# One written order for all engines and the loads, natural rows transposed by TensorE, and a shorter conversion of the weights

## The chip, the cores and the metric

The kernel runs on one core of a Trainium2 chip. The core has TensorE (PE in the profile, with its weight loads as PEld), VectorE (DVE), ScalarE (ACT), GpSimd (POOL) and SyncE (SP), which here only issues DMA transfers. The metric is the device time of one execution in microseconds (us), lower is better. A second execution with the hardware profiler gives the trace.

## The reference

Two attentions in a row, then a two-layer network with a softmax-weighted activation and a layer norm. B = 8 batches, H = 8 heads, S = 576 positions, D = 64, 32 packed rows of p for each head.

```python
def sm_attn(qq, kk, vv):
    s = scale * np.matmul(qq, kk.transpose(0, 1, 3, 2))
    s = s - np.max(s, axis=-1, keepdims=True)
    a = np.exp(s)
    a = a / (np.sum(a, axis=-1, keepdims=True) + 1e-09)
    return np.matmul(a, vv)
p_packed = sm_attn(p, k, v)
out = sm_attn(q, p_packed, p_packed)
# x: out with the heads side by side, 4608 tokens x 512
h = x @ w_in                       # 512 x 1024
e = np.exp(h - np.max(h, axis=-1, keepdims=True))
solu = h * (e / (np.sum(e, axis=-1, keepdims=True) + 1e-09))
ln = (solu - mean) / np.sqrt(var + 1e-06) * g_ln
return (ln @ w_out).astype(np.float32)   # 1024 x 512
```

`w_in`, `w_out` and `g_ln` are used here as they come: the two weight matrices lie in memory as float64, q, k, v, p and `g_ln` as float32. The output is float32.

## The kernel before

**Batches.** Each batch has two halves of attention. `pack(b)` (L342 on) computes the packed rows: k is transposed to `kT`, scores against p's transpose (L360 for batch 0, L368 later), softmax (L371 to L386), transposes of the weights `e1` by TensorE (L397), the product with v (L407, called PV here), the division by the row sums (`pp`, L411) and a transpose to `ppT` (L413, L415). `unpack(b)` computes the attention of q on those rows: q is transposed to `qT` (L428, by DVE in 32x32 blocks, or for batches 0 and 1 by TensorE in `transpose_rows`), scores (L457, L467), transposes of score blocks (L439), softmax (L443 to L451, two of its steps, L444 and L451, on POOL for b ≥ 1). The product with p's rows and the product with `w_in` are taken together: z = `ppT` times `w_in` (L483), split into a rounded part `zh` (L485) and the rest `zl` (L500, or for batch 0 L491 and L493 on ACT and POOL). The weights of the second attention are transposed (L505) and split the same way into `a2h` (L507) and `a2l` (L508).

**Token tiles.** 36 tiles of 128 tokens. `mlp_in` (L521) adds three products for each half (`a2h·zh + a2h·zl + a2l·zh`): 12 matmuls of 128x512, or 24 for the tile that lies across two batches. Then row maximum (L523), exponential (L531), `u` (L534); `mlp_norm` subtracts the mean (L542), writes `yhl` as two float16 parts (L544 on ACT, L545 on DVE), transposes them by DMA into `yT` (L547), and gets the row factor `c_row` (L549 to L555). `mlp_out` is 24 float16 matmuls into `po` (L564) with `w_out` as two float16 parts `wch` and `wcl`; the row and column factors go on in L566, and L571 stores.

**Weights.** Both matrices come as pairs of 32-bit words in chunks of 1 MB, four for each matrix. `high_part` (L202 on ACT, L204 and L205 on DVE) makes a float32 from the high words: the exponent is rebased by a scaling and a shift, and the sign bit is put back from the source by L205. `add_low_part` adds what the low words hold (L212 takes the power of two, L217, or L220 and L221, the product, L226/L227 or L233 the sum; a table `HOW` chooses engines for each of the eight chunks; in two ways, `3` and `6`, TensorE adds the parts in PSUM). For `w_out`, magnitudes are summed over rows (L301, L302), giving a power-of-two column scale (L307 to L311); each of eight chunks of 128 rows is multiplied by `g_ln` and that scale (L321, L322) and split into `wch` (L323) and `wcl` (L330).

**Loads.** Everything goes through SP's one queue. k of later batches is loaded in blocks with pieces of 128 bytes (L96), q in blocks too (L85); rows of k, q (batches 0 and 1) and v go in pieces of 512 bytes (L107) and a tail of 64 rows (L115 and its like). p is loaded in blocks twice: for batch 0 (L159; transposed by DVE, L261), and for the others (L167; transposed by DVE, L269, then four copies from SBUF to SBUF, L272).

**Start.** TensorE runs 12 small fp32 matmuls on ones (L248) and, at a few places, runs of 128x512 matmuls on ones (`keep_busy`, L255), 22 of which are before k's transposes.

**What sets the order.** For batches 1 to 7 TensorE's order is the order of the code, with positions taken from the tables `FIRST_BATCH` and `LATER` (`manual_schedule` for TensorE alone). All else is placed by a scheduler, which goes by estimated times and by the priority offsets in the tables at the top. Buffers: `raw` 3, `v_sb` 1, two each of `e`, `u`, `yhl`, `yT`, `o_sb`; PSUM 2 of `h`, 1 of `po`, 3 of `pa`.

## Time and profile before

| | |
|---|---|
| time, median of 3 runs | 469.91 us (468.54 to 470.03) |
| the profiled execution's own time | 468.75 us |
| its span in the trace | 466.9 us |
| PE busy | 429.6 us, 92% |
| DVE busy | 355.1 us, 76% |
| ACT busy | 231.2 us, 50% |
| POOL busy | 143.4 us, 31% |
| TensorE's mean granted clock | 0.952 |
| moved by DMA | 67.00 MB, 143 GB/s |

The shares are means over very different stretches: the page's slices show TensorE at 5 to 9 tenths in the first third and at 9 from then to the last slice, and DVE full from about the fifth slice to the tenth. The span is cut by stretch in the prediction. In a row of the trace, "x40" is the number of instructions of a group; an fp32 matmul leaves two records.

### The profile page before, as it was taken

The page shows a single profiled execution, that of the slowest core. Times are in us where ns is not written, and L with a number is a line of the kernel's source. Part 1 is how long each engine was busy: PE and PEld are TensorE (multiplying, and loading weights), DVE is VectorE, ACT ScalarE, POOL GpSimd, SP SyncE. Part 2 cuts the span into 40 slices and gives each one's busy share as a digit, 9 for nine tenths or more (in the row PEclk, how much of TensorE's full clock was granted, in tenths as well). Part 3 has the DMA queues.
Part 4 walks back from the last instruction along what each step waited for, and adds up shares of the span by engine and source line. Part 5 has one row for each costly group of instructions (what it writes and reads, how often), then busy time and mean ns, then how long its engine had stood idle before and what let it go on. Part 6 is the DMA issues. An engine that isn't in the chain of part 4 may idle for free.

```text
span 466.9 us, 8257 instructions
## 1 busy us (share of the span) xinstructions
PE 429.6 (92%) x3116; PEld 236.3 (51%) x3116; DVE 355.1 (76%) x649; ACT 231.2 (50%) x403; POOL 143.4 (31%) x243
## 2 busy tenths in 40 slices
...
GB/s 267 338 268 286 155 191 132 128 184 173 153 103 186 142 97 160 224 128 157 176 140 144 97 155 183 77 119 178 69 67 69 76 62 113 90 67 125 80 115 65
DMA packets 237880, 67.00 MB, mean 143 GB/s; under 512 B 208912, under 2 KB 231440, under 8 KB 237328
## 3 DMA queue, kind: packets, MB, share of 16 engines
...
q14 instruction: 16, 0.13, 0.1%
...
## 4 chain that ended last, share of the span: by engine, by line
PE 38%; DVE 31%; ACT 9%; issue 7%; DMA 7%; POOL 4%; SPq 2%; DVEq 0%; POOLq 0%; ACTq 0%
PE po L564 21%; PE h L521 12%; DVE nm L523 4%; ACT yhl L544 3%; DMA zh<-in_moe_w_in_dram 3%; DVE qT L428 3%; DVE kT L350 3%; DVE u L534 3%; DVE zl L500 3%; ACT e L549 2%; DVE yhl L545 2%; DVE mx L443 2%; DVE sm L448 2%; PE pa L407 1%; PE pa L467 1%
## 5 line engine op out<-in xcount | busy, mean ns | idle before, releaser
L564 PE MATMUL po<-wch,yT 128*128 128x512 f16 x576 | 182.7, 382 | 5.9 <-DVE o_sb L566 4.8
L564 PEld LDWEIGHTS <-yT 128*128 128x128 f16 x864 | 81.0, 98 | 115.2 <-issue 24.7
L564 PE MATMUL po<-wcl,yT 128*128 128x512 f16 x288 | 109.7, 381 | 0.0
L521 PE MATMUL h<-zh,a2h 128*128 128x512 f32 x160 | 70.2, 439 | 1.8 <-DVE u L534 1.5
L531 ACT ACTIVATE e<-h,nm 128x1024 f32<-128x1024 f32 x36 | 40.1, 1115 | 58.1 <-DVE nm L523 57.6
L544 ACT ACTIVATE yhl<-u,negmu 128x1024 f16<-128x1024 f32 x36 | 41.4, 1149 | 50.9 <-POOL negmu L542 47.2
L521 PE MATMUL h<-zh,a2l 128*128 128x512 f32 x160 | 64.4, 403 | 0.0
L521 PE MATMUL h<-zl,a2h 128*128 128x512 f32 x160 | 64.2, 401 | 0.0
L545 DVE SCALAR_TENSOR_TENSOR yhl<-u,negmu,yhl 128x1024 f16<-128x1024 f32 x36 | 46.4, 1288 | 17.4 <-ACT yhl L544 17.3
L534 DVE SCALAR_TENSOR_TENSOR u<-e,s_row,h 128x1024 f32<-128x1024 f32 x36 | 46.0, 1277 | 9.8 <-ACT e L531 8.6
L523 DVE TENSOR_REDUCE nm<-h 128x1 f32<-128x1024 f32 x36 | 43.6, 1212 | 11.7 <-PE h L521 11.6
L566 DVE SCALAR_TENSOR_TENSOR o_sb<-po,c_row,inv 128x512 f32<-128x512 f32 x36 | 26.8, 745 | 26.1 <-PE po L564 26.1
L551 POOL TENSOR_SCALAR s_eps<-se,s_row 128x1 f32<-128x1 f32 x36 | 10.7, 297 | 102.2 <-ACT e L531 65.3
L554 POOL TENSOR_SCALAR c_row<-sq,s_eps 128x1 f32<-128x1 f32 x36 | 15.7, 437 | 82.9 <-ACT e L549 82.9
L549 ACT ACTIVATE e<-u,negmu 128x1024 f32<-128x1024 f32 x36 | 40.9, 1136 | 0.0
L521 PEld LDWEIGHTS h<-zh,a2h 128*128 128x128 f32 x160 | 31.1, 194 | 18.9 <-issue 9.0
L521 PEld LDWEIGHTS h<-zh,a2l 128*128 128x128 f32 x160 | 30.8, 193 | 7.9 <-issue 0.5
L521 PEld LDWEIGHTS h<-zl,a2h 128*128 128x128 f32 x160 | 31.1, 194 | 6.0
L444 POOL TENSOR_TENSOR s<-s,mx 128x576 f32<-128x576 f32 x14 | 16.0, 1160 | 49.3 <-DVE mx L443 49.3
L446 ACT ACTIVATE a<-s 128x576 f32<-128x576 f32 x16 | 10.9, 684 | 30.6 <-POOL s L444 28.1
L508 DVE TENSOR_TENSOR a2l<-s,a2h 128x576 fp32r<-128x576 f32 x16 | 14.0, 881 | 13.1 <-ACT a2h L507 13.1
L381 ACT ACTIVATE e<-pa,nmx 128x288 f32<-128x288 f32 x28 | 13.7, 496 | 19.4 <-DVE nmx L373 10.8
(139 smaller groups left out, 614.1 us busy)
## 6 DMA issues: line engine op xcount, KB each, us to landing
...
```

What stands on the lines that cost most here:

```text
L350: nc.vector.transpose(out=kT[:, g], in_=kraw[:, g].rearrange('p a i -> p (a i)'))
L444: eng.tensor_tensor(out=s2[r], in0=s2[r], in1=mx.unsqueeze(2).broadcast_to([P, NB, J]), op=ALU.subtract)
L521: nc.tensor.matmul(h[:, 512 * n:512 * n + 512], lhsT=lhsT, rhs=z[:, r, 512 * n:512 * n + 512], start=t == 0, stop=t == len(terms) - 1)
L523: nc.vector.tensor_reduce(out=nm, in_=h, axis=AX.X, op=ALU.max, negate=True)
L531: nc.scalar.activation(e, h, AF.Exp, bias=nm, accum_out=se)
L534: nc.vector.scalar_tensor_tensor(out=u, in0=e, scalar=s_row, in1=h, op0=ALU.mult, op1=ALU.mult, accum_out=su)
L544: nc.scalar.activation(yhl[:, 0], u, AF.Identity, bias=negmu)
L545: nc.vector.scalar_tensor_tensor(out=yhl[:, 1], in0=u, scalar=negmu, in1=yhl[:, 0], op0=ALU.add, op1=ALU.subtract)
L549: nc.scalar.activation(e, u, AF.Square, bias=negmu, accum_out=sq)
L554: nc.gpsimd.tensor_scalar(out=c_row, in0=sq, scalar1=1.0 / DF, scalar2=s_eps, op0=ALU.mult, op1=ALU.add)
L564: nc.tensor.matmul(po, lhsT=yT[:, a, c], rhs=w[:, c], start=c == 0 and t == 0, stop=c == NFC - 1 and t == 2)
L566: nc.vector.scalar_tensor_tensor(out=o_sb, in0=po, scalar=c_row, in1=inv, op0=ALU.mult, op1=ALU.mult)
```

## The change

1. **One region with a written order.** All tables of offsets go. Every stage is a generator that emits one step at each call, and a string of about 1,300 names says which generator is called next. All engines, and SP's loads, follow that order. `Z` is the warm-up, `lk0` a load, `W0` and `O0` the conversion of a chunk, `S` the column scale, `C0` the scaled parts of a chunk, `k0` and `q0` the two halves of a batch, `z0` its z, `t0` a token tile.
2. **Natural rows.** k of batch 0 and q of batches 0 and 1 are loaded as rows with four positions of a head together (pieces of 1 KB), v of all batches as well; TensorE transposes k and q, and the two tails go by two 128x128 transposes. p is loaded once, as rows, and transposed by TensorE; ACT scales and copies it.
3. **Sign by slope.** `high_part` uses ACT's Prelu with a slope of 2^32 for negative inputs, so that one shift by DVE leaves the sign bit in place, and L205 falls away. The power of two for the low part comes from the same bits.
4. **Parts added by TensorE.** For all eight chunks of the conversion the low and high parts are added in PSUM (`whole`). Seven of the eight scaled chunks of `w_out` go from PSUM through one DVE instruction that applies `g_ln` and the column scale; the other takes ACT and POOL.
5. **Engines.** Tables choose POOL or DVE for the low products, the rests `zl`, `a2l`, `wcl` and two softmax steps. Runs of fill matmuls after the start are gone; the warm-up is 24 small and 15 large matmuls.

```diff
-HOW = '42313324'
-SCALED_BY = 'pppppdpp'
-REST_BY = 'pdddppdd'
+HOW = 'pddddddd'
+SCALED_BY = 'xxxxxxpx'
+REST_BY = 'ppppddpd'
+ZL_BY = 'ppdppdddpdpddddddddddddddddddddd'
+A2L_BY = 'pdpddpdddddddddd'
+SOFT_BY = 'dppppppppppppppp'
+KPE = '10000000'
+QPE = '11000000'
+ORDER = 'Z lk0 lw0 W0 W0 lw1 W0 lw3 lp lw2 W0 W0 lo1 lq0 lo0 k0 k0 k0 k0 k0 k0 k0 k0 k0 lo2 W1 W0 k0 p p p p p p p W2 ...
...
-    for _ in range(12):
-        ps = ps_a.tile([P, 512], F32, name='pa')
-        nc.tensor.matmul(ps[:, :P], lhsT=ones_f, rhs=ones_f, start=True, stop=True)
+    def warm_up():
+        for _ in range(24):
+            nc.tensor.matmul(spare[:, :P], lhsT=ones_f, rhs=ones_f, start=True, stop=True)
+        for _ in range(15):
+            nc.tensor.matmul(spare, lhsT=ones, rhs=ones.unsqueeze(1).broadcast_to([P, DM // P, P]), start=True, stop=True)
+        yield
...
+    def load_p():
+        raw = got['p'] = mlp.tile([P, DF], F32, name='e', bufs=2)
+        nc.sync.dma_start(raw[:, :ROWS // P * D], p.rearrange('b h t d -> (b h t) d')[:ROWS].rearrange('(p x) d -> p (x d)', p=P))
+        yield
+    def prepare_p():
...
+        for x0 in range(0, N, 4):
+            pt = ps_h.tile([P, DF], F32, name='h')
+            for x in range(x0, min(N, x0 + 4)):
+                for r in range(2):
+                    nc.tensor.matmul(pt[64 * r:64 * r + 64, (x - x0) * P:(x - x0 + 1) * P], lhsT=raw[:, x], rhs=ident, start=True, stop=True)
+            yield
+            n = min(N, x0 + 4) - x0
+            nc.scalar.activation(dst[:, x0:x0 + n], pt[:, :n * P].rearrange('p (x s) -> p x s', x=n), AF.Copy, scale=SCALE)
+            yield
...
     def high_part(dst, raw):
         bits = mlp.tile([P, DF], F32, name='e', bufs=2)
-        nc.scalar.activation(bits, hi.bitcast(F32), AF.Copy, scale=2.0 ** (-112))
-        bits = bits.bitcast(I32)
-        nc.vector.tensor_scalar(out=bits, in0=bits, scalar1=3, scalar2=2147483647, op0=ALU.logical_shift_left, op1=ALU.bitwise_and)
-        return nc.vector.scalar_tensor_tensor(out=dst.bitcast(I32), in0=hi, scalar=-2147483648, in1=bits, op0=ALU.bitwise_and, op1=ALU.bitwise_or)
+        nc.scalar.activation(bits, hi.bitcast(F32), AF.Prelu, scale=2.0 ** (-112), alpha=2.0 ** 32)
+        yield
+        nc.vector.tensor_scalar(out=dst.bitcast(I32), in0=bits.bitcast(I32), scalar1=3, scalar2=None, op0=ALU.logical_shift_left)
+        yield
+        return bits
+    def low_part(bits, raw, how, rest):
+        lo, _ = words_of(raw)
+        if how != 'd':
+            nc.scalar.activation(lo.bitcast(F32), lo.bitcast(U32), AF.Copy, scale=2.0 ** (-52))
+            yield
+        nc.vector.tensor_scalar(out=bits.bitcast(I32), in0=bits.bitcast(I32), scalar1=3, scalar2=-8388608, op0=ALU.logical_shift_left, op1=ALU.bitwise_and)
+        yield
+        if how == 'd':
+            nc.vector.scalar_tensor_tensor(out=rest, in0=lo.bitcast(U32), scalar=2.0 ** (-52), in1=bits, op0=ALU.mult, op1=ALU.mult)
+        else:
+            EN(nc, how).tensor_tensor(out=rest, in0=lo.bitcast(F32), in1=bits, op=ALU.mult)
+        yield
+    def whole(high, rest, i):
+        half = slice(512 * i, 512 * i + 512)
+        ps = ps_a.tile([P, 512], F32, name='pa')
+        nc.tensor.matmul(ps, lhsT=ident, rhs=high[:, half], start=True, stop=False)
+        nc.tensor.matmul(ps, lhsT=ident_r, rhs=rest[:, half], start=False, stop=True)
+        return ps
...
+    def scaled_parts(c):
+        n, i = c // 2, c % 2
+        w = wg[n][:, i * DM:(i + 1) * DM]
+        if SCALED_BY[c] == 'x':
+            ps = whole(wg[n], rests[n], i)
+            yield
+            nc.vector.scalar_tensor_tensor(out=w, in0=ps, scalar=g_sb[:, c:c + 1], in1=scale[0], op0=ALU.mult, op1=ALU.mult)
+        else:
+            EN(nc, SCALED_BY[c]).tensor_tensor(out=w, in0=w, in1=scale[0], op=ALU.mult)
+        yield
+        nc.scalar.copy(wch[:, c], w)
...
-    with tc.manual_schedule(engines={mybir.EngineType.PE}):
-        for b in range(1, B):
-            batch(b)
...
+    with tc.manual_schedule():
+        for name in ORDER.split():
+            next(flows[name], None)
```

What stands where on the engines before and after, at three places. In these rows a line number is that of the kernel's own source, a number behind a name tells buffers apart, and "x4" means four alike in a row.

TensorE at the start, before: the warm-up on ones (L248), the fill matmuls (L255), k's transposes (L125, L127).

```order
L248 MATMUL pa<-ones_f 128x128 x3
L255 MATMUL po<-ones 128x512 x15
L248 MATMUL pa<-ones_f 128x128 x3
L255 MATMUL po<-ones 128x512 x7
L125 MATMUL h<-ident,raw 64x128 x6
L248 MATMUL pa<-ones_f 128x128 x3
L125 MATMUL h<-ident,raw 64x128 x4
L127 MATMUL h<-ident,raw 128x64
```

The same place after: the warm-up (L92, L94), k's transposes (L293, L299), sums of parts of `w_in` (L203 and L204 are the two matmuls of `whole`), p's transposes (L162).

```order
L92 MATMUL po<-ones_f 128x128 x24
L94 MATMUL po<-ones 128x512 x15
L293 MATMUL h<-ident,raw 64x128 x32
L299 MATMUL h<-ident,raw 128x128 x2
L203 MATMUL pa<-w_in_sb,ident 128x512
L204 MATMUL pa<-u,ident_r 128x512
L162 MATMUL h<-ident,e 64x128 x32
```

The warm-up now stands in one piece ahead of k's transposes, and a part of `w_in` and all of p stand between these and batch 0's scores (L324, nine rows further on).

VectorE around the column scale, before: L307 to L311 compute the scale from the sums of magnitudes in `po`; L371 and L373 are batch 1's softmax maxima, L508 is `a2l` of batch 0.

```order
L350 STREAM_TRANSPOSE kT<-raw 128x576 x4
L217 SCALAR_TENSOR_TENSOR u<-raw,u 128x1024
L508 TENSOR_TENSOR a2l_183<-s_532,a2h_182 128x576
L508 TENSOR_TENSOR a2l_183<-s_536,a2h_182 128x576
L307 TENSOR_SCALAR o_sb<-po 128x512
L371 TENSOR_REDUCE mx_718<-pa 128x1 x2
L371 TENSOR_REDUCE mx_737<-pa 128x1
L308 TENSOR_SCALAR o_sb<-o_sb 128x512
L373 TENSOR_REDUCE nmx<-mx_718 128x1
L310 TENSOR_SCALAR o_sb<-o_sb 128x512
L311 TENSOR_SCALAR inv<-o_sb 128x512
L322 TENSOR_TENSOR yT<-yT,o_sb 128x512
```

After: L245 to L250 are the scale, L259 the scaled chunks that DVE reads from PSUM, L306 transposes of k of batch 1, L437 of batch 0's weights, L466 the last `zl` on DVE.

```order
L466 TENSOR_TENSOR zl<-h,zh 128x512
L437 STREAM_TRANSPOSE s_621<-a_564 128x576
L245 TENSOR_SCALAR o_sb<-po 128x512
L246 TENSOR_SCALAR o_sb<-o_sb 128x512
L248 TENSOR_SCALAR o_sb<-o_sb 128x512
L250 TENSOR_SCALAR inv<-o_sb 128x512
L259 SCALAR_TENSOR_TENSOR yT<-pa,g_sb,o_sb 128x512
L306 STREAM_TRANSPOSE kT<-raw 128x576 x2
L259 SCALAR_TENSOR_TENSOR yhl<-pa,g_sb,o_sb 128x512
L259 SCALAR_TENSOR_TENSOR yT<-pa,g_sb,o_sb 128x512
```

The four steps of the scale stand together now, and the scaling that was POOL's (seven of eight L322) is in DVE's list between them and batch 1.

SP's first loads, before: w (`zh`, `zl`, L138), p of batch 0 (L159), rows of k (L107, L115) and v.

```order
L138 DMA zh<-in_moe_w_in_dram 128x2048
L159 DMA o_sb<-in_p_dram 32x4x32 x4
L107 DMA raw<-in_k_dram 128x8x128 x2
L115 DMA raw<-in_k_dram 64x4x64 x2
L138 DMA zl<-in_moe_w_in_dram 128x2048
L107 DMA v_sb<-in_v_dram 128x8x128 x2
L134 DMA v_sb<-in_v_dram 64x8x64
L138 DMA zh<-in_moe_w_in_dram 128x2048
L138 DMA zl<-in_moe_w_in_dram 128x2048
L107 DMA raw<-in_q_dram 128x8x128 x2
```

After: k first (L102, L110), then w (L139), p whole (L149), and v of batch 0 behind q and three chunks of `w_out`.

```order
L102 DMA raw<-in_k_dram 128x8x256
L110 DMA raw<-in_k_dram 64x4x64 x2
L139 DMA zh<-in_moe_w_in_dram 128x2048
L139 DMA zl<-in_moe_w_in_dram 128x2048 x2
L149 DMA e<-in_p_dram 128x1024
L139 DMA zh<-in_moe_w_in_dram 128x2048
L139 DMA zh<-in_moe_w_out_dram 128x2x1024
L102 DMA raw<-in_q_dram 128x8x256
L110 DMA raw<-in_q_dram 64x4x64 x2
L139 DMA raw<-in_moe_w_out_dram 128x2x1024 x2
L102 DMA v_sb<-in_v_dram 128x8x256
```

`v` has moved from fourth to eleventh place, k to the first.

More of the change, by code (lines that the diff above doesn't have):

```diff
@@ L189, in packed_attention_solu_kernel @@
     wcl = const.tile([P, NFC, DM], F16, name='wcl')
[L191 to L233 removed]
+    inv = const.tile([P, DM], F32, name='inv')
     ident = const.tile([P, P], F32, name='ident')
@@ new lines, in packed_attention_solu_kernel, with raw_tile @@
+    got, packed, wg, rests, sums, scale = ({}, {}, {}, {}, [], [])
+    spare = ps_o.tile([P, DM], F32, name='po')
+    def warm_up():
[4 more added lines that the diff above has]
+        yield
+    def raw_tile():
+        return raws.tile([P, G, NB, 32], F32, name='raw', bufs=3)
@@ new lines, in whole, with convert_w_in @@
+    def whole(high, rest, i):
[4 more added lines that the diff above has]
+        return ps
+    def convert_w_in(g):
+        bits = yield from high_part(w_in_sb[:, g], got[f'w{g}'])
+        rest = mlp.tile([P, DF], F32R, name='u', bufs=2)
+        yield from low_part(bits, got[f'w{g}'], HOW[g], rest)
+        for i in range(2):
+            ps = whole(w_in_sb[:, g], rest, i)
+            yield
+            nc.scalar.copy(w_in_sb[:, g, 512 * i:512 * i + 512], ps)
+            yield
@@ L565, in mlp_out @@
         o_sb = mlp.tile([P, DM], F32, name='o_sb', bufs=2)
         nc.vector.scalar_tensor_tensor(out=o_sb, in0=po, scalar=c_row, in1=inv, op0=ALU.mult, op1=ALU.mult)
-        stores.append((out[row:row + P, :], o_sb))
-    def store():
-        while stores:
-            nc.sync.dma_start(*stores.pop(0))
-    def run(work, n=None, offset=0):
-        with tc.high_priority(offset=offset):
-            for _ in range(n or 99):
-                next(work, None)
-    work = pack(0)
-    for offset in PACK0:
-        run(work, 1, offset)
@@ L602, in packed_attention_solu_kernel @@
-    for what in 'kvq':
-        prefetch(1, what, 0)
-    pack1 = pack(1)
-    keep_busy(*BUSY[3])
-    normed, summed, stores = ([], [], [])
-    def step(row, parts, knobs, work):
-        lag, pout, pnorm = knobs
-        before, after, mid = work
-        before()
-        nxt = mlp_in(row, parts)
-        after()
-        ready = normed.pop(0) if len(normed) > lag else None
-        if summed:
-            with tc.high_priority(offset=pnorm):
-                normed.append(mlp_norm(*summed.pop()))
-        store()
-        if ready:
-            with tc.high_priority(offset=pout):
-                mlp_out(*ready, mid)
-        else:
-            for i in range(3):
-                mid(i)
-        summed.append(nxt)
@@ L627, in batch @@
-    def batch(b):
-        ui, pi, qi, (pun, patt), order, pfirst = FIRST_BATCH if b == 0 else LATER[(b - 1) % 2] if b < B - 1 else LATER[2]
-        second = unpack(b + 1) if b + 1 < B else iter(())
-        first = pack(b + 2) if b + 2 < B else iter(())
+        yield
+        nc.sync.dma_start(out[row:row + P, :], o_sb)
+        yield
+    flows = {'Z': warm_up(), 'p': prepare_p(), 'S': column_scale(), 'lp': load_p(), 'lg': load_g()}
+    for i in range(4):
+        flows[f'W{i}'] = convert_w_in(i)
+        flows[f'O{i}'] = convert_w_out(i)
+        flows[f'lw{i}'] = load_w('w', i)
+        flows[f'lo{i}'] = load_w('o', i)
@@ L636, in more @@
-        def more(n):
-            if n in qi:
-                run(pack1, qi.count(n), pfirst)
-            if n in ui:
-                run(second, ui.count(n), pun)
-            if n in pi:
-                run(first, pi.count(n), patt)
-        def at(i):
-            return (lambda: more(5 * i), lambda: more(5 * i + 1), lambda j: more(5 * i + 2 + j))
-        for i, (row, parts) in enumerate(tiles):
-            if b == 0:
-                keep_busy(*BUSY[4 + i])
-            for what, when, offset in FETCH[0 if b == 0 else 1 if b == 1 else 2]:
-                if when == i:
-                    prefetch(b + 2, what, offset)
-            step(row, parts, order, at(i))
@@ L653, in batch @@
[L653 to L664 removed]
+            flows[f't{n}'] = token_tile(n, b * S + i * P + (LEFT if odd else 0), [(odd, i * P + (P if odd else 0))])
```

549 lines of the change are left out of this document (221 added, 328 removed).

## The prediction

> **What bounds the kernel now.** I read the busy time by stretch first. Its columns are the stretch and its length in us, then busy time and count for PE, PEld, DVE, ACT and POOL, the granted TensorE clock, the DMA share and GB/s.
>
> ```profile
> 0.00:40.00 40.00, 34.16 (x333) 23.94 (x334) 21.51 (x39) 22.16 (x42) 11.54 (x16) 0.91 0.97 280
> 40.00:126.82 86.82, 67.36 (x457) 33.90 (x456) 77.81 (x117) 51.32 (x91) 48.55 (x44) 0.82 1.17 172
> 126.82:160.00 33.18, 28.91 (x248) 15.77 (x246) 22.80 (x49) 12.97 (x25) 5.50 (x12) 0.90 0.88 145
> 160.00:440.00 280.00, 277.82 (x1987) 152.42 (x1987) 223.28 (x432) 138.94 (x239) 73.82 (x163) 1.00 0.63 120
> ```
>
> From 160 to 440 TensorE is busy 277.82 of 280 us at a clock of 1.00: nothing is to be had there, and the change leaves those matmuls as they are. The tail behind it has the same last tiles. What can move is the first third. There DVE is the full engine: 77.81 of 86.82 us between 40 and 126.82. The chain of waits (start, length, what) shows which work that is, and the timeline of TensorE shows where it ends:
>
> ```profile
> 66.46 2.80 POOL yT L233
> ...
> 75.60 4.49 POOL yT L322 x3
> ...
> 413.69 5.20 PE po L564 x24
> ```
>
> ```profile
> 126.82 0.58 PE L521 MATMUL h<-zh,a2h 128*128 128x512 f32 x1
> ```
>
> The first two pieces are the middle of the chain, the conversion of `w_out` on POOL: its sums (L233) and its scaling (L322), which the first token tiles wait for. The third is one tile's `mlp_out` late in the run, where TensorE follows TensorE. I cut the run at 126.82, the first matmul that reads batch 1's `a2h`: before it TensorE mostly waits for what DVE and POOL prepare, after it it mostly works. I call that point X. In the written order of the changed kernel, the same matmul has 60 matmuls of `mlp_out` before it where this one has had 67; every other matmul ahead of it is the same work. So the sum is: DVE's work to X, plus its idle time to X, plus what is left after X.
>
> **DVE's work up to X.** Now 21.51 + 77.81 = 99.3 us. The rows (min/median/max or busy and mean in ns) that price what goes and comes:
>
> ```profile
> L205 DVE SCALAR_TENSOR_TENSOR w_in_sb<-zl,e 128x1024 int32<-128x1024 int32 x2 | 2.5, 1226 | 0.1
> ...
> L217 DVE SCALAR_TENSOR_TENSOR u<-zl,u 128x1024 f32<-128x1024 uint32 x1 | 1.2, 1225 | 0.0
> ...
> L221 DVE TENSOR_TENSOR u<-u 128x1024 f32<-128x1024 f32 x2 | 3.5, 1764 | 0.1
> ...
> L566 DVE SCALAR_TENSOR_TENSOR o_sb<-po,c_row,inv 128x512 f32<-128x512 f32 x36 | 26.8, 745 | 26.1 <-PE po L564 26.1
> ...
> L322 DVE TENSOR_TENSOR yT<-yT,o_sb 128x512 f32<-128x512 f32 x1 | 1.8, 1773 | 0.0
> ...
> L500 DVE TENSOR_TENSOR zl<-pa,zh 128x512 fp32r<-128x512 f32 x4 | 2.6, 682 | 1.0 <-ACT zh L485 1.0
> ...
> L428 DVE STREAM_TRANSPOSE qT<-raw 128x576 f32<-128x576 f32 x4 | 2.7, 734 | 0.0
> ...
> L545 DVE SCALAR_TENSOR_TENSOR yhl<-u,negmu,yhl 128x1024 f16<-128x1024 f32 x4 | 5.4, 1353 | 4.8 <-ACT yhl L544 4.8
> ...
> L269 DVE STREAM_TRANSPOSE p2t<-p2raw 128x896 f32<-128x896 f32 x1 | 1.1, 1111 | 0.8 <-ACT p2raw L267 0.8
> ...
> L508 DVE TENSOR_TENSOR a2l<-s,a2h x16: 731/746/2898, 66.3 to 415.3; 128x576 fp32r<-128x576 f32 x16
> ...
> L330 DVE TENSOR_TENSOR wcl<-yhl,wch x4: 674/1164/1429, 78.2 to 93.5; 128x512 f16<-128x512 f32 x4
> ```
>
> - Sign by slope: the eight L205 go, 8 × 1.22 = −9.8. A Prelu takes the place of the Copy on ACT, off the path (51 of 86.8 us busy); no row shows its time, and I take the Copy's, about 1.15. Twice that would add 9 us to ACT, which has over 30 to spare.
> - Low parts: seven products come to DVE and two L217 and two L221 go: 7 × 1.22 − 2 × 1.22 − 2 × 1.2 (L221 at L217's time for the same size; the rest of its 1.76 counts as contention) = +3.7.
> - Scale: seven of eight chunks are now one DVE instruction that reads the sum in PSUM. No row shows it; the nearest is L566, with the same tile, two factors and a PSUM input, 0.745. 7 × 0.75 − 0.75 for the one L322 that DVE had = +4.5. If it took L205's 1.22 it would be +3.3 more; both ends are kept.
> - `wcl` from five on DVE to three, 2 × 0.67 (L330's shortest) = −1.3; two L451 to POOL, 2 × 0.75 as L508's median for a tile of the same size, −1.5; `a2l` and `zl` of the first two batches, four of eight to POOL, −1.5 − 1.4; `p` no longer transposed here −1.7 (1.11 and two small ones); `minus_r` −0.3.
> - Moved behind X: batch 2's four q transposes, 4 × 0.73 = −2.9, and one L545, −1.3.
>
> Sum −13.5 us. The second saving is contention. Some of DVE's rows are stretched where POOL works at the same time:
>
> ```profile
> 40.00:97.00 57.00, 41.73 (x292) 22.86 (x291) 54.33 (x73) 37.20 (x68) 39.22 (x28) 0.76 1.17 171
> ...
> L204 DVE TENSOR_SCALAR e<-e x8: 653/694/2350, 7.5 to 50.5; 128x1024 int32<-128x1024 int32 x8
> ...
> L205 DVE SCALAR_TENSOR_TENSOR yT<-raw,e x2: 1224/2209/3194, 33.7 to 46.1; 128x1024 int32<-128x1024 int32 x2
> ...
> L449 DVE TENSOR_SCALAR sm<-sm x16: 131/164/1721, 54.2 to 379.6; 128x18 f32<-128x18 f32 x16
> ```
>
> Longest less median for L204, L508 and L449, longest less shortest for L205, and four times median less shortest for L330: 1.66 + 2.15 + 1.56 + 1.97 + 1.96 = 9.3 us, beside 39.2 us of POOL between 40 and 97, or 0.24 us for each us of POOL. The change takes the products L221, sums L233 and seven L322 off POOL and leaves or brings:
>
> ```profile
> L493 POOL TENSOR_TENSOR zl<-o_sb,zh 128x512 fp32r<-128x512 f32 x4 | 6.2, 1566 | 1.8 <-ACT o_sb L491 1.8
> ...
> L330 POOL TENSOR_TENSOR wcl<-yT,wch 128x512 f16<-128x512 f32 x3 | 3.9, 1314 | 0.1
> ...
> L451 POOL TENSOR_TENSOR a<-a,sm 128x576 f32<-128x576 f32 x14 | 16.1, 1159 | 5.6 <-DVE sm L450 3.1 <-DVE s_row L528 2.3
> ```
>
> 4 × 1.57 (zl) + 5 × 1.31 (wcl) + 3 × 1.16 (two of the softmax, one `a2l`) + one scale of about 1.7 = 18 us. At 0.24 that stretches DVE by 4.3 instead of 9.3: −5.0. **Work to X: 99.3 − 13.5 − 5.0 = 80.8 us.** What is late next is again DVE, whose list is shorter but still the longest: TensorE's work to X is 101.5 us at mixed clocks, but a good part of it is fill and half-clock time.
>
> The Trainium skill ("SBUF — State Buffer", SBUF: two separate sides) says that VectorE and GpSimd share one pair of SBUF ports as an exclusive lock, and the loser waits for the whole of the other's instruction. The longest L205 agrees (1.97 us over its time); the average of 0.24 does not say that each POOL instruction costs that.
>
> **DVE's idle time to X.** Now 18.5 us before 40 and 9.0 after. DVE cannot run ahead of the first batch's attention, so its early idle time is set by when that ends. TensorE's rows at the start (start, length; an fp32 matmul has two records):
>
> ```profile
> 1.12 1.65 PE L248 MATMUL pa<-ones_f 128*128 128x128 f32 x6 [1.12 <-POOL neg_half L259]
> 2.42 5.78 PE L255 MATMUL po<-ones 128*128 128x512 f32 x15
> 8.04 0.83 PE L248 MATMUL pa<-ones_f 128*128 128x128 f32 x6
> 8.62 1.87 PE L255 MATMUL po<-ones 128*128 128x512 f32 x7
> ...
> 15.99 1.09 PE L125 MATMUL h<-ident,raw 128*64 128x128 f32 x16
> 17.22 2.10 PE L360 MATMUL h<-kT,pT 64*32 64x288 f32 x32
> ...
> 23.46 3.00 PE L397 MATMUL pa<-ident,e 128*128 128x128 f32 x10 [4.14 <-ACT e L381]
> ...
> 33.88 1.02 PE L226 MATMUL pa<-w_in_sb,ident 128*128 128x512 f32 x2
> ...
> 51.92 2.06 PE L226 MATMUL pa<-yhl,ident 128*128 128x512 f32 x2
> ```
>
> ```profile
> 31.40 0.48 DVE L411 TENSOR_SCALAR pp<-pa,rs 128x64 f32<-128x64 f32 x2
> ```
>
> `pp` of batch 0 is done at 31.9. The new order puts all 24 small and 15 large warm-up matmuls first, at about 0.47 us a small one while the clock is low and 0.20 after (a group's time less some 0.23 for its end), 0.25 a large one. With the clock low to about 7.5, as the first 15 large ones show at 0.385 each, they are through at 13. Then k's transposes 4 × 1.09 + 0.3 to 17.7, half a part sum 1.02, p's transposes 4 × 1.09 to 23.1, four more part sums 4.1 to 27.2, the scores 2.1, the softmax of the second half 4.1, and transposes, PV and `pp` in 5.8 (23.46 to 31.88 now, less 2.6 of q's transposes among them): **39 instead of 31.9**. DVE's work placed ahead of that point is 12.2 us (22 rows), so it idles 26.8 there. For the waits behind it I take 7 of the 9.0, since the order now lists `zl`, a slower POOL hand-over, in the same places. X = 80.8 + 26.8 + 7 = 114.6.
>
> One load can set the 39. v0 comes after 11.4 MB of k, w, p and q on SP's one queue:
>
> ```profile
> 10.00:12.00 2.00, 2.00 (x21) 1.44 (x19) 1.31 (x2) 0.00 (x0) 0.50 (x1) 1.00 0.96 397
> ```
>
> At the 280 GB/s of the first 40 us it lands at 41 and PV is some 5.5 late; at the 397 that the wide pieces of w reach, it lands at 29. k, q and v now have pieces of 1 KB instead of 512 B; I take about 34, in time, and keep +5.5. SP also puts v1, k1, q1 behind v0; v1 waits until PV has freed the one `v_sb`, and behind it stand k1, q1, k2 and the first `yT`. PV ends at 39 and the first `yT` is wanted 30 us later, so no engine waits for that queue.
>
> **After X.** 466.9 − 126.82 = 340.1 now. Seven more matmuls of `mlp_out` are left, 7 × 0.217 = +1.5 (24 take 5.20 in the steady state). Between 126.82 and 160 TensorE idles 4.3 us and runs at 0.90 (about 2.7 more); with more tiles ready I take 3 of it back. 340.1 + 1.5 − 3 = 338.6. Span 114.6 + 338.6 = 453.2, and with the 1.85 that the profiled execution has around its span (468.75 against 466.9): **455 us**. That execution is 1.2 under the median of 469.91, which is left in the range.
>
> **Rivals.**
>
> Steady state loses. The hand-written order now also covers SP, DVE, ACT and POOL, where before only TensorE's was written. A late entry holds all behind it on its engine. Batch 1 of before shows such gaps:
>
> ```profile
> 137.58 1.73 PE L407 MATMUL pa<-v_sb,e1T 128*32 128x64 f32 x80 [1.51 <-ACT e1T L398]
> ...
> 140.95 0.45 PE L413 MATMUL pa<-ident,pp 128*128 128x128 f32 x1 [1.64 <-DVE pp L411]
> ```
>
> One such wait a batch, 1.5 × 6 = 9, gives about 464.5 (461 to 471). Against it speaks that TensorE's own list was already written there and lost only 2.2 of 280.
>
> Slower: the clock. One mechanism, from the column scale on. TensorE's granted clock was half through stretches of full work:
>
> ```profile
> 65.00:70.00 5.00, 5.00 (x24) 1.81 (x18) 5.00 (x5) 0.71 (x2) 2.80 (x1) 0.50 0.99 117
> ```
>
> The change gives TensorE seven more pairs of part sums and drops the later fill matmuls. If it stays at half clock for the 25 us behind the scale, the part sums cost 8 × 1.04 more (L226: 2.06 against 1.02), the first two tiles 24 × 0.22, the transposes and scores of batch 1 about 5.5 (k's and q's transposes and scores above, at twice their time): 19, of which some 2 are in gaps, so 455 + 17 = 472 (470 to 476). It decides if the low clock holds over 25 us. The Trainium skill ("TensorE: Matmul & The Clock Gate", Part 1: The HAM clock gate) has full speed return after about 3.4 us of sustained work, which would make this cost under 2 us. The 5 us above, full and at 0.50, do not bear that out.
>
> The lock, in full. If every POOL instruction of the 18 us held DVE up for its whole length, X would be 14 later: about 469, no change. Speaking against it: 0.24, measured over 39 us. [...]
>
> More gained. No contention at all (−4.3) and the waits of 7 near 2: about 446. The order brings DVE less to wait for, but nothing in the trace shows so clean a start.
>
> **How the numbers follow.** Forecast 455 (448 to 462) 0.47; more gained 0.13; steady state loses 0.18; lock 0.05; clock 0.17. The bounds of the unknown operations, +3.3 for the scale, +5.5 for v0, ±4 for waits, lie in 448 to 462. The range reaches from 444 to 472, which leaves out half of the clock's case and the ends of the others. A measurement tells some 0.3% apart, 1.4 us. Faster: 0.47 + 0.13 + 0.15 = 0.75; same: 0.05 + 0.03 of the steady-state case = 0.08; slower 0.17.
>
> **What the profile will show.** Right: `pp` of batch 0 done near 39; DVE busy about 81 us up to the first matmul on batch 1's `a2h`, which starts near 115; the scale by DVE at 0.75 us a chunk; 160 to 440 full as before. Wrong: a row of 0.50 clock from the scale to that point with TensorE full (clock); gaps of over 1 us at every batch behind 160 (steady state); DVE rows near the scale at twice their median (lock); or DVE idle over 10 us between `pp` and X, which would mean that another engine or a load, not DVE, sets that stretch.

## The result, and the profile after

| | before | after |
|---|---|---|
| median | 469.25 us (468.54 to 470.03, 4 runs) | 454.53 us (453.93 to 455.57, 4 runs) |
| span of the profiled execution | 466.9 us | 452.9 us |
| TensorE's mean granted clock | 0.952 | 0.984 |
| first matmul on batch 1's `a2h` (point X) | 126.82 us | 115.26 us |

The ratio of after to before is 0.9688, with a 95% interval of 0.9661 to 0.9716: 3.1% faster, at the time that was forecast (455.0). The sum was right, and two of its terms were not: one was off by 6.5 us and one by 7.1, in opposite directions. Most of what follows is about those two.

Busy time by stretch, after (columns as in the prediction). The first two rows are cut where `pp` of batch 0 is done and at X:

```profile
0.00:38.57 38.57, 34.74 (x377) 26.80 (x379) 11.69 (x26) 24.29 (x36) 5.35 (x13) 0.96 0.94 324
38.57:115.26 76.69, 64.97 (x515) 33.12 (x511) 62.61 (x116) 46.84 (x80) 26.30 (x34) 0.93 0.76 121
115.26:160.00 44.74, 43.38 (x356) 24.31 (x356) 38.16 (x77) 24.61 (x47) 13.13 (x21) 1.00 0.88 147
160.00:426.00 266.00, 262.11 (x1892) 143.88 (x1891) 221.04 (x409) 130.04 (x221) 80.93 (x155) 1.00 0.67 131
```

The same cut of before:

```profile
0.00:31.88 31.88, 26.45 (x282) 20.13 (x284) 16.72 (x32) 15.62 (x32) 10.75 (x15) 0.89 0.97 289
31.88:126.82 94.94, 75.08 (x513) 37.72 (x510) 82.60 (x124) 57.87 (x101) 49.34 (x44) 0.84 1.15 178
```

The reader sees three things. Batch 0's attention ends 6.7 us later than before. The stretch from there to X is 18.3 us shorter, and in it VectorE has 20.0 us less to do (82.60 to 62.61) and GpSimd about half (49.34 to 26.30). Behind X, what is left is 340.1 us before and 337.6 after, 2.5 less, where 1.5 less was forecast.

The timeline of the changed kernel: VectorE at `pp`, TensorE at the tile that lies across batches 0 and 1, ScalarE where it writes batch 1's first `a2h`:

```profile
38.10 0.47 DVE L371 TENSOR_SCALAR pp<-pa,rs 128x64 f32<-128x64 f32 x2 [3.72 <-PE pa L367]
```

```profile
113.68 0.58 PE L479 MATMUL h<-zh,a2h 128*128 128x512 f32 x1
...
115.26 0.40 PE L479 MATMUL h<-zh,a2h 128*128 128x512 f32 x1
```

```profile
114.43 0.67 ACT L440 CAST a2h<-s 128x576 fp32r<-128x576 f32 x1 [1.12 <-DVE s L437]
```

The first six matmuls of that tile's first half read batch 0's part. So the row at 113.68, ahead of the `a2h` written at 114.43, is not X; X is the seventh, at 115.26. The expectations on the runs below take 113.7 for it. I call the tile's first matmul Y. In the written order Y comes 1.6 us ahead of X in the changed kernel and in every run, so the runs are compared at Y.

And the groups of VectorE that answer to the ones priced in the prediction (count, busy us and mean ns):

```profile
L259 DVE SCALAR_TENSOR_TENSOR yT<-pa,g_sb,o_sb 128x512 f32<-128x512 f32 x4 | 3.0, 742 | 0.0
...
L194 DVE SCALAR_TENSOR_TENSOR u<-zh,e 128x1024 fp32r<-128x1024 uint32 x2 | 2.4, 1224 | 0.1
...
L406 DVE TENSOR_SCALAR sm<-sm 128x18 f32<-128x18 f32 x4 | 2.1, 536 | 0.1
...
L272 DVE TENSOR_TENSOR wcl<-yT,wch 128x512 f16<-128x512 f32 x2 | 1.4, 678 | 0.0
```

The scale from PSUM takes 0.742 us (0.75 was taken), the low product 1.224, `wcl` 0.678. Of the groups up to X, L406 is the one that is still far above its own shortest time (0.176). The rows of before that were stretched beside GpSimd, some 15 us over their own time up to X, are nearly gone.

### The profile page after: what moved, and what is told of

It is laid out like the page before. It is cut to its first block, busy times and chain, and to the rows that moved or that the text cites. A ratio compares the mean times of both kernels' runs of the same rounds, so it can differ in the third digit from the quotient of the medians.

```text
span 452.9 us, 8367 instructions
## 1 busy us (share of the span) xinstructions
PE 425.7 (94%) x3221; PEld 237.0 (52%) x3221; DVE 342.7 (76%) x637; ACT 231.7 (51%) x393; POOL 132.6 (29%) x238
## 4 chain that ended last, share of the span: by engine, by line
PE 53%; DVE 27%; ACT 4%; issue 3%; POOL 1%; DVEq 0%; ACTq 0%; POOLq 0%
PE po L521 28%; PE h L479 16%; DVE u L495 4%; DVE yhl L503 4%; DVE nm L482 4%; PE pa L455 3%; DVE o_sb L525 2%; PE pa L425 2%; DVE sm L405 2%; DVE mx L397 2%; DVE zl L466 2%; DVE sm L406 1%; PE pa L324 1%; DVE s L437 1%; PE pa L367 1%
## 5 line engine op out<-in xcount | busy, mean ns | idle before, releaser
L479 PE MATMUL h<-zh,a2l 128*128 128x512 f32 x160 | 63.2, 395 | 0.8 <-POOL a2l L442 0.8
L479 PE MATMUL h<-zl,a2h 128*128 128x512 f32 x160 | 62.6, 391 | 0.0
L498 POOL TENSOR_SCALAR negmu<-su 128x1 f32<-128x1 f32 x36 | 7.6, 211 | 148.5 <-DVE u L495 148.5
L458 ACT CAST zh<-pa 128x512 fp32r<-128x512 f32 x28 | 16.2, 586 | 41.8 <-PE pa L455 41.8
L409 POOL TENSOR_TENSOR a<-a,sm 128x576 f32<-128x576 f32 x16 | 20.9, 1312 | 15.1 <-DVE sm L407 7.1
L516 POOL TENSOR_TENSOR c_row<-c_row,neg_half 128x1 f32<-128x1 f32 x36 | 23.9, 665 | 3.0
```

The lines of the kernel that those rows point to most:

```text
L409: EN(nc, SOFT_BY[2 * b + 1]).tensor_tensor(out=w2, in0=w2, in1=sm.unsqueeze(2).broadcast_to([P, NB, J]), op=ALU.mult)
L458: nc.scalar.copy(z_h[:, r, cols], pz)
L479: nc.tensor.matmul(h[:, 512 * n:512 * n + 512], lhsT=lhsT, rhs=z[:, r, 512 * n:512 * n + 512], start=t == 0, stop=t == len(terms) - 1)
L516: nc.gpsimd.tensor_tensor(out=c_row, in0=c_row, in1=neg_half, op=ALU.pow)
```

## The experiments

All compare with the changed kernel (454.5 us, span 452.9) and were timed beside the kernel before; a ratio is to that. From `pp` to Y the changed kernel shows:

```profile
38.57:113.68 75.11, 63.39 (x508) 31.91 (x505) 61.73 (x115) 46.16 (x79) 25.07 (x32) 0.93 0.77 124
```

Theory A: VectorE's list behind `pp` sets this stretch. Theory B: the written order does, and VectorE has room. Theory C: GpSimd's part does, by its length in the chain and by holding VectorE up. Theory D: the end of batch 0's attention does.

### The sign put back by its own instruction

```diff
-        nc.scalar.activation(bits, hi.bitcast(F32), AF.Prelu, scale=2.0 ** (-112), alpha=2.0 ** 32)
+        nc.scalar.activation(bits, hi.bitcast(F32), AF.Copy, scale=2.0 ** (-112))
...
-        nc.vector.tensor_scalar(out=dst.bitcast(I32), in0=bits.bitcast(I32), scalar1=3, scalar2=None, op0=ALU.logical_shift_left)
+        nc.vector.tensor_scalar(out=bits.bitcast(I32), in0=bits.bitcast(I32), scalar1=3, scalar2=2147483647, op0=ALU.logical_shift_left, op1=ALU.bitwise_and)
+        nc.vector.scalar_tensor_tensor(out=dst.bitcast(I32), in0=hi, scalar=-2147483648, in1=bits.bitcast(I32), op0=ALU.bitwise_and, op1=ALU.bitwise_or)
```

(and the power of two taken from `dst`, as before the change.)

> The changed kernel (454.5 us) with the sign put back by an instruction of its own on VectorE, eight times 1.22 us; the order and all else stay. Four of the eight stand ahead of batch 0's pp, where VectorE idles 26.9 us, four behind it. Theory A (VectorE's list behind pp sets the stretch up to the first matmul on batch 1): about 4 x 1.22 = +4.9, so 458 to 460, with that matmul near 118.5 instead of 113.7. Theory B (the written order made the gain, VectorE has room: it idles 13.4 us in that stretch): within 1.4 us of 454.5.

Measured: 459.9 us, ratio 0.9807 (0.9779 to 0.9835). The stretch from `pp` to Y, in that run:

```profile
39.93:117.94 78.01, 63.11 (x508) 32.14 (x505) 67.01 (x117) 46.33 (x79) 25.13 (x32) 0.91 0.73 119
```

VectorE does 5.3 us more there (67.01 against 61.73), and the stretch is 2.9 longer. Y is 4.3 later, of which 1.4 come from a later `pp`; behind Y it takes 1.2 more, and the whole run 5.4. The time is what theory A said, and B is out for this list; but only 2.9 of the 5.3 us of added work lengthened the stretch. So the sign by slope is worth some 5 us of the 14.7.

### The scaling of `w_out` back on GpSimd

```diff
-SCALED_BY = 'xxxxxxpx'
+SCALED_BY = 'pppppppp'
```

(In the order, the sum of parts and its copy stand where the seven chunks had their sum.)

> The changed kernel with the column scale of all eight chunks on GpSimd, after a copy by ScalarE, instead of seven on VectorE from PSUM. VectorE loses 7 x 0.74 = 5.2 us, GpSimd gets 7 x 1.8 = 12.6 us, ScalarE 7 copies. Theory A with the forecast's 0.24 us of stretch for each us of GpSimd: -5.2 + 3.0, so about 452 to 453. Theory C (GpSimd's time beside VectorE, and its length in the chain of w_out, was most of what the change removed): 457 to 461.

Measured: 464.05 us, ratio 0.9893 (0.9865 to 0.9921), above both expectations. From `pp` to Y:

```profile
37.90:121.60 83.70, 67.19 (x509) 33.34 (x505) 59.15 (x106) 50.25 (x86) 33.82 (x39) 0.90 0.69 111
```

VectorE has 2.6 us less to do than in the changed kernel (59.15 against 61.73), and the stretch is 8.6 us longer. So VectorE's work is not what sets it alone: in this run it is idle for 24.5 us of the stretch. Where the time goes is seen on TensorE and ScalarE, which wait for GpSimd's scaling and for the buffers that it frees:

```profile
82.58 1.49 PE L203 MATMUL pa<-yhl,ident 128*128 128x512 f32 x2 [3.79 <-ACT yT L238]
```

```profile
80.80 0.62 ACT L263 CAST wch<-yhl 128x512 f16<-128x512 f32 x1 [4.33 <-POOL yhl L261]
```

ScalarE stands for 4.33 us at a chunk that GpSimd has not scaled, the next chunk's copy is behind it, and TensorE's next sum of parts waits for that. What the direct route from PSUM bought is a chain with one hand-over fewer (TensorE, VectorE, ScalarE instead of TensorE, ScalarE, GpSimd, ScalarE) and buffers that come free earlier, more than it cost VectorE. Theory C, in its first half.

### The low products back on GpSimd

```diff
-HOW = 'pddddddd'
+HOW = 'pppppppp'
```

(The order has one entry more for each of the seven chunks, for ScalarE's copy.)

> The changed kernel with all eight low products on GpSimd behind a copy by ScalarE (one is there now). VectorE loses 7 x 1.22 = 8.5 us, of which 5 behind pp; GpSimd gets 7 x 2.4 = 17 us, ScalarE 7 x 1.15. Theory A with 0.24: -6.1 + 2.9 behind pp, about 451 to 453. Theory C: the product is slower by 1.2 and one hand-over longer at each chunk, and VectorE's rows beside it are stretched again to 2 to 3 us: 457 to 463.

Measured: 472.24 us, ratio 1.0075 (1.0047 to 1.0104): with this one table the whole gain is gone. `pp` is done at 48.8 instead of 38.6, since the sums of parts of `w_in` stand ahead of batch 0's scores on TensorE and come late; VectorE waits for these scores:

```profile
37.23 0.82 DVE L328 TENSOR_REDUCE mx<-h 128x1 f32<-128x288 f32 x2 [11.94 <-PE h L324]
```

From `pp` to Y it is 7.1 us longer, with VectorE's list shorter (59.40). It says again that the length of the chain over the engines counts. It does not measure what the low products cost in before, where another order stood around them.

### Only TensorE's order written

```diff
-    with tc.manual_schedule():
+    with tc.manual_schedule(engines={mybir.EngineType.PE}):
```

> The changed kernel's instructions, but only TensorE's order is the written one; the other engines and the loads are placed by the scheduler, as before the change. Theory A (less work on VectorE makes the gain): 453 to 457. Theory B (the order of the other engines makes it): at least half of the gain is lost, 462 to 470.

Measured: 521.17 us, ratio 1.1116 (1.1086 to 1.1147), far beyond what was expected. TensorE is slack even late: 257.99 of 280 us busy from 240 on. Without its tables of offsets the scheduler makes an order that, it seems, does not fit TensorE's; which rows cost the time was not followed up. The run shows that the order of the other engines matters a great deal for these instructions. It is no undo of that part of the change, for the order of before had its own tables, and what the written order alone is worth against that one stays open.

### Two buffers for the magnitudes

```diff
-            mag = mlp.tile([P, DM], F32R, name='mag', bufs=1)
+            mag = mlp.tile([P, DM], F32R, name='mag', bufs=2)
```

> The changed kernel with two buffers for the magnitudes of w_out instead of one. In its trace the last three sums wait 2.93, 0.81 and 0.81 us for ScalarE's magnitude, and each magnitude for the sum before it, between 50.6 and 57.3 us; TensorE falls to half clock there. If this ping-pong is on the chain: the sums end about 1.5 us earlier, less half clock behind them, 452 to 453.5. If VectorE's shift of the last chunk (52.2 us) or the scale's place in VectorE's order holds them anyway: 454 to 455.

Measured: 453.49 us, ratio 0.9679 (0.9637 to 0.9720), profiled span 450.3. From `pp` to Y it takes 73.38 instead of 75.11. (`pp` itself was 0.85 earlier in this profile, which the edit does not reach: TensorE's granted clock from 32 to 36 us was 1.00 here and 0.57 in the changed kernel's profile.) The direction is as expected for the ping-pong; the interval does not tell it from the changed kernel.

### The scores of batch 0 ahead of the parts of `w_in`, first try

```diff
-p p p p p p p W2 W0 W0 W0 W1 W1 lv0 p W1 W1 W1 W1 W1 W2 W2 W2 lo3 W3 W2 k0 k0 W2 k0 k0 k0 k0
+p p p p p p p p W0 W1 W1 lv0 W1 k0 W2 W0 W0 W1 k0 W1 k0 W1 W1 k0 k0 k0 W2 W2 W2 lo3 W3 W2 W2
```

> The changed kernel with the scores of batch 0 moved ahead of four sums of parts of w_in on TensorE, and the last copy of p's transpose ahead of two copies of these on ScalarE. Theory D (the end of batch 0's attention gates all that follows; the change made pp 6.7 us later than before): pp near 35 instead of 38.6, and the end 3 us earlier, about 451.5. Theory A (VectorE's list behind pp, with the conversion of w_out in it, sets it): 453.5 to 454.5, since that list gets no shorter, or 453 if the whole list starts earlier.

Measured: 459.14 us, ratio 0.9790 (0.9752 to 0.9827). The first half of the scores was earlier, but the order put chunk 2's preparation behind both maxima on VectorE, so that a sum of parts held TensorE:

```profile
31.96 1.10 PE L203 MATMUL pa<-w_in_sb,ident 128*128 128x512 f32 x2 [1.85 <-DVE w_in_sb L181]
```

`pp` came at 43.3 instead of 38.6. As an improvement it failed; as a test it is clean: `pp` 4.7 later, the stretch to Y unchanged (75.25 against 75.11), the span 4.8 longer. A late batch 0 goes to the end one for one.

### A shorter warm-up

```diff
-        for _ in range(15):
+        for _ in range(4):
```

> The changed kernel with 4 large warm-up matmuls instead of 15, 11 x 0.245 = 2.7 us less ahead of k's transposes. If the warm-up's length is on the path to pp: up to 1.8 us earlier (p lands near 16.2, its transposes now begin at 18.0), so about 452.7 to 454. If the granted clock falls without it, k's and p's transposes take up to twice their 4 us: 455 to 458.

Measured: 455.51 us, ratio 0.9708 (0.9670 to 0.9747): no difference. TensorE is ahead up to PV, and then a load holds it:

```profile
35.05 1.95 PE L367 MATMUL pa<-v_sb,e1T 128*32 128x64 f32 x80 [1.62 <-DMA v_sb<-in_v_dram]
```

v lands at 35.0. In the changed kernel it is issued at 20.9, lands 14.7 us later, at 35.6, and PV starts at 36.30 without a wait: it has 0.7 us to spare.

### GpSimd kept busy beside the conversion

```diff
+        junk = const.tile([P, DM], F32, name='junk')
+        for _ in range(14):
+            nc.gpsimd.tensor_tensor(out=junk, in0=wg[0][:, :DM], in1=wg[0][:, :DM], op=ALU.mult)
```

(And fourteen entries in the order, between two steps of batch 0's second half.)

> The changed kernel with 14 products of 128x512 on GpSimd that nothing needs, from about 39 us on, where GpSimd stands idle up to 57.8 us: 17 us of GpSimd beside VectorE's conversion work. Nothing waits for them but GpSimd's own next step. By the forecast's 0.24 us of stretch for each us of GpSimd: +4, about 458.5. If each of VectorE's instructions between tiles in SBUF waits for a whole one of GpSimd's (14 such there, up to 1.2 each): +8 to +12, 463 to 467. If there is no contention: 454.5.

Measured: 459.66 us, ratio 0.9805 (0.9767 to 0.9843), span 457.1, +4.2, near the +4 of the forecast's rate. From `pp` to Y it is 4.9 us longer (80.06), with 7.0 more for VectorE. GpSimd's row, one of its fourteen products, and VectorE's rows beside them (start, length):

```profile
38.57 20.97 POOL L244 TENSOR_TENSOR junk<-yT 128x512 f32<-128x512 f32 x14 [24.08 <-DVE yT L181]
...
50.27 1.37 POOL L244 TENSOR_TENSOR junk<-yT 128x512 f32<-128x512 f32 x1
```

```profile
45.10 1.64 DVE L194 SCALAR_TENSOR_TENSOR u<-raw,e 128x1024 fp32r<-128x1024 uint32 x1
46.66 0.47 DVE L399 STREAM_TRANSPOSE s<-h 128x288 f32<-128x288 f32 x1
47.06 1.36 DVE L403 TENSOR_REDUCE mx<-s 128x18 f32<-128x576 f32 x2
...
49.22 1.52 DVE L181 TENSOR_SCALAR yT<-e 128x1024 int32<-128x1024 int32 x1
50.67 2.05 DVE L194 SCALAR_TENSOR_TENSOR u<-zh,e 128x1024 fp32r<-128x1024 uint32 x1
52.65 3.10 DVE L405 TENSOR_TENSOR s<-s,mx 128x576 f32<-128x576 f32 x2
```

The changed kernel's own rows for the last two kinds:

```profile
49.75 1.22 DVE L194 SCALAR_TENSOR_TENSOR u<-zh,e 128x1024 fp32r<-128x1024 uint32 x1
50.88 1.42 DVE L399 TENSOR_TENSOR s<-s,mx 128x576 f32<-128x576 f32 x2
```

The shift goes from 0.69 to 1.52, the low product from 1.22 to 2.05, a subtraction from 0.71 to 1.55. The transposes out of PSUM and the reductions keep their 0.47 and 0.68 a piece. Up to 60 us the stretched rows sum to 6.8 us beside 21 us of GpSimd, 0.32 us for each; GpSimd's products took 1.50 on average, from 1.04 to 1.95. So contention is real, falls on some operations alone, and costs the run most of what it adds to VectorE.

How much is added follows from the product under way. One ran from 50.27 to 51.64; the low product that began beside it, at 50.67, ended at 52.72 and needs 1.22 alone, so it got going at 51.50, 0.14 us before the product's end. Every stretched row here fits this. So do 14 stretched rows of the kernel before, up to X: each got going 0.1 to 0.2 us before the end of the GpSimd instruction that it had found running. The longest of them, GpSimd first:

```profile
45.82 2.38 POOL L221 TENSOR_TENSOR u<-u 128x1024 fp32r<-128x1024 f32 x1 [1.27 <-DVE mx L443]
```

```profile
46.08 3.19 DVE L205 SCALAR_TENSOR_TENSOR yT<-raw,e 128x1024 int32<-128x1024 int32 x1
```

GpSimd is done at 48.20, and 49.27 less the 1.22 of this instruction is 48.05. A row of these kinds waits for the rest of the one GpSimd instruction that it finds running, and GpSimd waits in turn: its products took 1.04 where no such row held them, 1.37 and more beside one. So 0.24 or 0.32 for each us of GpSimd is a mean over chance meetings and not a rate.

The Trainium skill ("SBUF — State Buffer", Who interferes with whom) names the same two kinds, instructions with two inputs in SBUF and `tensor_scalar` in a fast mode, leaves out reductions, and lets whichever comes first hold the shared ports for its whole instruction. The trace agrees in all three, but for the 0.1 to 0.2 us at the end.

### Zeros instead of products

```diff
-            nc.gpsimd.tensor_tensor(out=junk, in0=wg[0][:, :DM], in1=wg[0][:, :DM], op=ALU.mult)
+            nc.gpsimd.memset(junk, 0.0)
```

(Against the run with products; the fourteen entries stand at the same place in the order.)

> The changed kernel with 14 writes of zeros to the unused tile on GpSimd, where the run with 14 products read a tile of SBUF. The products stretched VectorE's rows beside them up to twice and cost 5 us. If it is GpSimd's reading that holds VectorE up: the two-input rows (the low product, the softmax subtraction) keep their 1.22 and 0.71 us and the time is 454.5, or 456 if the shifts alone are held by the writes. If any work of GpSimd does: 457 to 460.

Measured: 454.58 us, ratio 0.9719 (0.9690 to 0.9747). This tells little: with nothing to read, the writes ran from 14.5 to 23.4 us, ahead of the stretch meant. Beside them stood one shift (0.78 for 0.69), one mask (0.90 for 0.69) and one low product, which kept its 1.22.

### Putting the best together

```diff
-p p p p p p p W2 W0 W0 W0 W1 W1 lv0 p W1 W1 W1 W1 W1 W2 W2 W2 lo3 W3 W2 k0 k0 W2 k0 k0 k0 k0 W2 q0 k0
+p p p p p p p p W0 W1 W1 lv0 lo2 W1 W2 k0 k0 W2 W2 k0 k0 k0 k0 W2 k0 W0 W0 W1 W1 W1 W1 lo3 W3 q0
...
```

(The rest of chunk 2's sums follow behind the transposes of batch 0's weights; `lo2`, the load of a chunk of `w_out`, stood ahead of these entries.)

> The changed kernel with both score groups of batch 0 right behind p's transposes, ahead of five sums of parts of w_in, the softmax ahead of their copies on ScalarE, and v of batch 0 ahead of one chunk of w_out in the loads. The reordering before moved pp 4.7 us later and the end 4.8 later. Theory D (pp's time goes to the end one for one, and v lands in time when it is asked for earlier): pp near 34.5 instead of 38.6, the end 3.5 to 4.5 us earlier, 450 to 451. Theory A' (VectorE's and ScalarE's conversion of w_out behind pp takes over as soon as pp is earlier): less than 1.5 us, 453 to 454.5.

Measured: 454.44 us, ratio 0.9717 (0.9692 to 0.9742): nothing. `pp` is 1.3 us earlier, and its transpose on TensorE is not:

```profile
40.50 0.27 PE L374 MATMUL pa<-ident,pp 128*128 128x128 f32 x1
```

In the changed kernel that row starts at 40.56. It stands behind q's transposes, so their end and not `pp` opens what follows. Theory D needs this correction: a late `pp` costs, and an early one does not pay while q's transposes stay where they are.

Then with the short warm-up and the second buffer, both edits as above:

> As the kernel before in this list, with 4 large warm-up matmuls instead of 15 and two buffers for the magnitudes. Each alone gave -0.9 and -2.6 us of span at most. Theory D: pp another 1.5 earlier unless v's load holds it, and 2 from the magnitudes: 446.5 to 449. Theory A': 451 to 453.

Measured: 452.0 us, ratio 0.9670 (0.9638 to 0.9702), not to be told from the changed kernel's 0.9688. Y came at 112.60, `pp` at 37.3 as without the short warm-up. Last, z's second half moved ahead of the first sum of parts of `w_out`:

```diff
-z0 z0 C0 lv1 z0 z0 z0
+z0 z0 lv1 z0 z0 C0 z0
```

> The last combination (452.0 us; scores of batch 0 first, short warm-up, two buffers for the magnitudes) with the second half of batch 0's z ahead of the first sum of parts of w_out on TensorE. In the changed kernel's trace that sum (57.9 to 60.2, at half clock) stands ahead of z, and VectorE waits 1.90 us for z ahead of the column scale. If that wait is on the chain: the scale about 2 us earlier, 450 to 451. If VectorE's list up to there is full anyway (in the last trace it does not wait there any more): 451.5 to 452.5.

Measured: 451.42 us over 5 runs, ratio 0.9624 (0.9596 to 0.9652): faster than both kernels, 0.6% less than the changed one, with intervals that just miss each other. Its interval overlaps that of the run before it. Y is at 111.38, 1.2 earlier than there, but the move of z does not show in it:

```profile
35.73:111.38 75.65, 64.78 (x517) 32.97 (x516) 61.51 (x113) 46.28 (x80) 25.41 (x32) 0.93 0.78 126
```

From `pp` to Y it takes 75.65 us, where the run before took 75.32; what is earlier is `pp`, 35.7 instead of 37.3, with the same order up to it, and pp's transpose with it (38.96 instead of 40.51). TensorE's granted clock from 14 to 19 us was 0.66 in the profile of the run before and 1.00 in this one. So the edits of the last three runs together make a kernel that is faster than the changed one; that z's move gained anything is not shown. It ran without a repeat of the changed kernel beside it, so the size of the gain is the least certain number here.

## Why the prediction was right, and where it was not

| term | forecast | measured |
|---|---|---|
| `pp` of batch 0 done | 39 | 38.6 |
| VectorE idle ahead of it | 26.8 | 26.9 |
| VectorE's work up to X | 80.8 | 74.3 |
| VectorE idle between `pp` and X | 7 | 14.1 |
| X | 114.6 | 115.3 |
| after X | 338.6 | 337.6 |
| span | 453.2 | 452.9 |

**The cut at X held.** What is left behind Y was 339.2 us in the changed kernel. In the eleven other kernels with the whole order written it was 339.1 to 339.4 in ten and 340.5 in one, that with the sign put back. In these, TensorE's saturated part and its tail hardly noticed what was done ahead of it, so a change at the start can be priced by this point alone. With TensorE's order alone written it was 373.8: there the cut does not hold.

**The start held.** The warm-up ended at 12.0 (13 was taken), p's transposes at 22.2, `pp` at 38.6. v landed at 35.6 where 34 was taken; the 280 GB/s that would have put it at 41 did not come, as the slices of the first 34 us moved near 340 GB/s.

**VectorE's work was 6.5 us less than forecast**, and the step that failed is the one on contention: "Work to X: 99.3 − 13.5 − 5.0 = 80.8 us." The 9.3 us of stretched rows counted there were not all. More were in rows of before such as these:

```profile
L212 DVE TENSOR_SCALAR u<-yT x2: 695/1230/1766, 41.6 to 59.2; 128x1024 int32<-128x1024 int32 x2
L212 DVE TENSOR_SCALAR u<-yhl x2: 680/871/1062, 53.6 to 61.5; 128x1024 int32<-128x1024 int32 x2
...
L385 DVE TENSOR_SCALAR rs<-ssum x8: 156/165/955, 25.6 to 360.0; 128x2 f32<-128x2 f32 x8
```

That is 1.4 + 0.8 us; with L322 (1.773 for 0.68), the fifth L330 (1.680 for 0.68), L221 and two small ones it makes about 15. After, it is 1.6, nearly all in L406. So contention gave some 13 us, not 5.0, and the work itself about 12 of the 25.0, where 13.5 was forecast. The fall is steeper than GpSimd's (49.34 to 26.30 from `pp` to X), because what begins beside GpSimd now is mostly transposes and reductions, the kinds that the run with 14 products left alone, and the scale from PSUM, which keeps its 0.74. Only three rows up to X met a GpSimd instruction and waited. The rate of 0.24 for each us was a mean over a mixture that the change altered; that the run with 14 products came near it is luck.

**VectorE's waits were 7.1 us more than forecast.** The step was "For the waits behind it I take 7 of the 9.0". The 9.0 were counted from 40 us on and not from `pp`: between `pp` and X, VectorE of the kernel before idles 94.94 − 82.60 = 12.3 us. After, it is 76.69 − 62.61 = 14.1. So 3.3 of the 7.1 us were lost in the counting, and the waits rose by 1.7 where they were to fall by 2.

The forecast's own sign, more than 10 us idle there, was met by the kernel before as well, so by itself it does not say that something else has taken over. Over the whole change VectorE's list paid nearly in full: 20.0 us less work, a stretch 18.3 shorter. That the list alone does not set the stretch is shown by the scaling run, with less work for VectorE and 8.6 us more. The rest is waiting for a chain that goes through VectorE, ScalarE and TensorE in turn:

```profile
50.65 0.49 PE L229 MATMUL po<-mag,ones 128*128 128x512 f32 x1 [1.23 <-ACT mag L225]
54.08 0.79 PE L229 MATMUL po<-mag,ones 128*128 128x512 f32 x1 [2.93 <-ACT mag L225]
55.68 0.80 PE L229 MATMUL po<-mag,ones 128*128 128x512 f32 x1 [0.81 <-ACT mag L225]
57.29 0.79 PE L229 MATMUL po<-mag,ones 128*128 128x512 f32 x1 [0.81 <-ACT mag L225]
57.88 1.91 PE L203 MATMUL pa<-yT,ident 128*128 128x512 f32 x2
```

TensorE waits for magnitudes, VectorE then for z and the scale; with two buffers for the magnitudes the stretch was 1.7 us shorter. Work added to VectorE costs about half to three quarters of its time in the stretch (the sign 2.9 of 5.3 us, the 14 products 4.9 of 7.0). Work handed to GpSimd came back as hand-overs and more. The two errors have causes of their own, stretched rows left out of one count and waits left out of another. That they cancelled to less than 1 us at X is luck.

**The rivals.** *The clock* came up, at a small price. TensorE idled at 50 to 57 us, and the next rows ran at half: 57.88 above, 1.91 for what takes 1.02.

```profile
58.00:60.00 2.00, 2.00 (x4) 0.55 (x2) 1.97 (x4) 1.25 (x3) 1.73 (x2) 0.50 1.03 333
60.00:62.00 2.00, 2.00 (x17) 0.23 (x16) 0.90 (x2) 0.00 (x0) 2.00 (x3) 0.50 1.34 241
62.00:64.00 2.00, 2.00 (x12) 1.07 (x5) 1.17 (x2) 1.03 (x2) 0.82 (x1) 0.74 0.87 76
```

From 57.3 on TensorE is full, and the clock is back at 63 (0.74 over the 2 us from 62): some 5.7 us at half, about 2.9 us lost, not the 17 of the rival, which needed it over 25 us. In the kernel before, the row of 65 to 70 that the prediction shows goes on:

```profile
70.00:75.00 5.00, 5.00 (x23) 3.87 (x21) 4.96 (x10) 3.86 (x10) 2.49 (x2) 0.50 1.55 140
```

The Trainium skill's 3.4 us ("TensorE: Matmul & The Clock Gate", Part 1: The HAM clock gate) is nearer to the 5.7 us than to these 10 us full at 0.50 before the change. *The lock in full* did not come as it was priced: 26 us of GpSimd from `pp` to X stretched VectorE by 1.6. Not the wait was wrong in that rival, for a row that meets GpSimd waits out its instruction, but that every GpSimd instruction would be met by such a row. *The steady state* lost a little: 3.9 us of 266 idle where it was 2.2 of 280. Most of it is one wait, for the instruction that frees `po`; over the whole run it grew from 4.8 to 6.8 us:

```profile
L521 PE MATMUL po<-wch,yT 128*128 128x512 f16 x576 | 182.7, 380 | 7.2 <-DVE o_sb L525 6.8
```

It was paid back between X and 160, where TensorE idles 1.4 us of 45 instead of 4.3 of 33, at a clock of 1.00 instead of 0.90.
